# Cosine attention and a highway layer on one core: a new order of the same operations

## The chip, the cores and the metric

The kernel runs on one core of a Trainium2 chip. The metric is the device time of one execution in microseconds (us); smaller is better.

## What is computed

Eight batches, twelve heads, 448 tokens, head width 64. Queries and keys are brought to unit length, the scores divided by `tau` (0.1), and softmax attention gives `x` of 3584 x 768. A highway layer follows.

```python
q_n = q / (np.linalg.norm(q, axis=-1, keepdims=True) + 1e-06)
k_n = k / (np.linalg.norm(k, axis=-1, keepdims=True) + 1e-06)
scores = np.matmul(q_n, k_n.transpose(0, 1, 3, 2)) / tau
attn = softmax(scores)
x = (attn @ v).transpose(0, 2, 1, 3).reshape(3584, 768)
H = np.maximum(x @ w_h, 0.0)
T = 1.0 / (1.0 + np.exp(-(x @ w_t + b_t)))
out = T * H + (1.0 - T) * x
```

## The kernel before

The twelve heads of a batch are worked on as six pairs (head p and head p+6). Pair p of batch b has the number s = 6b + p, from 0 to 47. The first 384 tokens of a head are its main part, the last 64 its tail. The names below are those that the code gives its operations; a reader needs them to follow the steps.

**Loads.** `ld6 qr b` and `ld6 kr b` (L315) bring the main part of a whole batch of q or k, cast to fp16, 576 KB in SBUF; they are issued by GpSimd on the software queue. Batch 0 comes in pieces on the same queue: `ld2` (pairs 1 and 2, 96 KB, two for q and two for k) and `ld3` (pairs 3 to 5, 144 KB, again four; both L322). Pair 0 has loads of its own on SP and ScalarE (`ldf`, `ldqa`, `ldka`; L301 to L309). The tails of q, k and v are `ldqt`, `ldkt`, `ldvt` (L330, L334, L340; two halves of 96 KB each), and `ldv` (L338) is the main part of v, 1152 KB; SP issues them, and ScalarE issues the two `ldkt` of batch 0. `ld wt`, `ld wh` and `ld b` (L345, L347) are the weights and the bias, on the software queue.

**Attention.** Squares of q and k (`sq2`, `sq3`, of the tails `sqt`; on ScalarE L374 and L400, from batch 1 on with the main part on DVE, L375) are folded on DVE (`fa`, `fb`, `fc`; L389, L391, L393), and two Newton steps (`nt`, seven instructions, L423 to L429) give the inverse lengths. GpSimd scales q and k of a pair (`qn s`, `kn s`, L493) and the tails of q (`qtn b`, L503); DVE scales the tails of k (`kb`, L512). PE transposes a pair (`turn s`, L528 to L533) and the tails (`tail3 b`, L548), DVE copies them from PSUM (`cpT s` L537, `cpt3 b` L552). Of the scores PE makes three chunks of the main keys (`qk s c`, L582) and one of the tails (`qkt s`, L595), ScalarE the exponentials (`exp s c` L588, `expt s` L599). Values are cast to fp16 by `vc b p` (L607) and, the tails, by `vtc b` (L613, two halves, on ScalarE). PE multiplies (`av s c`, `avt s`; L625 to L645), DVE divides (`rc s` L653, `ev s` L655) into `x`. Pair 0 of batch 0 has its own small versions of these steps (`first_pair`, names with `0 0`).

**Highway layer.** Four row groups g = 4b + i to a batch. `x` is transposed by the DMA engines (`xd6`, `xd3`, L677, issued by SP) in batches 1 to 6, and by PE (`xt6`, L682, with DVE's `cpx6`) in the first and the last. `ff4` and `ff3` are groups of matmuls with the bias and the two weights (L702 to L716); ScalarE does `th` (L730), DVE `hm`, `gt`, `gg` (L737, L744, L747), GpSimd the last sum `out` (L752; DVE in the last two groups), and SP stores (`st`, `sth`; L762, L758). Twenty `warm2` (L283) are two matmuls each on constants, whose result nothing reads.

**What sets the order.** Nothing is scheduled at run time. `plan` collects 1807 operations in the order of the code; the table `ORDER` is a permutation of them, and each engine runs its own in that order. `SLOTS` gives, for each buffer at its first use, its place in a ring (three for `qr`, `kr`, two for `kt`, `qt`, `vt`, `vr`, four PSUM banks `pB`, two `pS`). `URGENT` marks operations of GpSimd on which the next marked operation of DVE waits, since the two share a port. A wait follows from data, from a buffer that must be free, and from the semaphores of the transfers: the transfers of SP and ScalarE together have eight, those of GpSimd eight more, in turn, so that a transfer waits in its engine's queue until the eighth before it has landed.

PE runs three kinds of tile: whole ones, the 64-row tiles of `qk`, and the 64-column tiles of the last row group of a batch.

Of the kernel before, what the change touches and what calls it, by code (L numbers as in the profile page):

```python
# [20 lines left out]
19 16 15 25 18 17 4 20 21 26 23 22 3 27 1 35 28 13 296 39 31 11 34 5 10 40 30 33 41 24 42 29 43 2 32 44 102 7 0  # L21
90 45 57 46 47 291 96 48 49 9 50 91 51 8 292 59 87 52 60 53 101 58 38 54 97 6 36 61 99 89 37 85 62 94 63 92 293
88 12 294 64 65 66 56 67 68 69 55 70 71 112 103 295 106 86 113 130 110 108 109 111 107 129 14 117 72 298 121 104
119 105 118 73 131 122 299 95 120 74 98 132 115 149 116 75 140 93 516 148 134 138 76 114 100 139 77 150 133 521
78 190 124 141 123 79 80 126 152 135 125 81 171 136 82 297 151 137 168 127 153 128 159 167 154 155 144 300 169
156 142 170 186 157 160 145 143 305 209 513 317 172 306 178 83 158 146 187 147 179 161 307 514 163 173 301 188
176 308 174 302 177 84 518 189 205 175 309 193 303 164 194 191 304 206 162 197 192 318 207 198 310 195 208 180
515 196 311 165 216 319 212 217 200 312 320 213 210 181 313 321 201 211 214 166 199 202 215 314 183 322 315 182
203 316 204 334 337 517 218 184 219 220 323 185 221 329 222 223 336 332 260 324 242 355 261 224 333 262 243 729
331 263 244 325 330 264 247 225 732 356 338 326 229 728 327 339 520 248 328 374 230 249 343 393 341 344 357 226  # L30
432 358 342 227 375 231 235 228 245 431 378 366 246 376 413 367 364 377 345 412 236 346 433 238 414 522 527 365
381 434 250 394 237 528 251 944 382 532 347 232 415 335 362 360 529 340 233 736 252 348 265 530 731 256 363 234
385 730 395 533 386 266 519 361 523 352 253 396 397 379 383 359 534 349 380 254 531 350 524 733 384 368 370 535
369 351 435 255 400 267 417 239 271 418 525 371 257 390 401 272 536 258 387 353 416 398 273 402 399 526 734 389
388 268 240 354 403 436 391 372 269 392 437 404 537 442 270 405 440 419 538 748 443 278 408 441 406 539 409 540
407 541 423 420 279 438 542 410 280 543 411 439 552 281 373 550 551 421 447 424 445 545 446 422 444 546 283 282
448 544 553 555 449 426 612 554 425 571 549 547 427 548 428 742 570 560 429 743 558 430 284 559 589 450 572 285
561 590 556 573 562 557 948 738 591 581 467 737 563 577 579 593 592 564 627 580 565 1160 567 600 739 943 566 259
582 575 735 286 601 747 460 951 578 454 568 744 484 740 574 461 741 609 770 455 650 462 950 468 608 631 569 576
469 287 610 949 749 470 596 598 611 597 451 288 452 750 764 477 751 628 453 478 599 963 457 629 808 274 745 615  # L40
630 594 646 616 458 479 471 647 746 595 459 947 472 1158 752 765 584 753 501 953 586 473 585 474 846 754 275 456
619 755 583 620 475 756 757 827 758 634 476 613 276 635 648 587 488 649 614 604 588 605 766 602 638 632 639 759
617 603 633 489 786 606 945 607 494 618 289 463 495 767 490 651 496 636 491 761 637 1159 657 464 762 492 652 763
785 640 493 655 958 653 760 656 624 623 480 642 1162 952 658 768 622 946 654 769 621 842 643 1161 641 625 865
771 644 824 775 241 645 787 776 662 843 788 777 659 772 660 626 804 661 485 778 663 805 664 796 773 797 665 954
794 806 774 962 486 1165 844 795 807 823 781 682 779 845 782 465 780 809 783 790 784 502 791 481 503 789 1178
505 810 506 955 504 964 813 699 792 487 825 1168 793 672 965 686 1023 497 957 1177 687 814 673 507 482 966 811
688 849 812 798 826 815 800 959 799 850 483 508 669 1167 466 816 290 670 960 1163 674 979 801 862 666 1164 498
667 1169 671 675 668 509 689 956 499 676 961 690 716 802 803 832 830 833 510 683 691 500 677 700 831 861 511 847
1080 967 1374 692 968 1042 678 701 969 1172 1179 703 1373 848 970 1180 684 1173 971 1170 693 702 972 1174 704  # L50
685 973 694 980 863 1000 1181 834 705 709 981 864 851 828 1171 852 817 982 710 976 835 820 819 829 853 975 706
711 707 854 1378 974 818 985 1377 708 868 1001 872 821 869 1595 855 983 679 873 866 984 1039 870 867 858 822 856
1020 837 977 871 839 978 857 1038 1002 859 838 860 1019 986 990 1003 987 836 992 1057 840 876 841 874 991 877
1058 875 993 1007 878 1005 680 879 1008 1040 1021 880 1041 1006 1059 1011 1382 1009 1238 897 717 1219 712 1060
1010 1076 718 1022 720 512 719 1077 1166 721 1004 713 1012 1024 914 988 1175 1025 1078 1392 881 1079 1295 277
714 1016 989 1376 722 1015 1030 1176 1375 1047 1388 1049 1014 695 681 1589 1050 1013 715 882 1017 1048 1182 1018
890 1588 1031 696 1045 1043 1183 1046 995 723 1383 918 1044 994 1184 1393 997 996 883 919 1394 884 920 1384 1194
1064 1066 1185 1276 885 1186 1067 1187 887 998 999 888 1065 1188 724 898 1385 886 891 1196 1028 892 1026 725
1029 899 1386 915 900 1197 889 1027 1068 916 1191 904 1200 1395 1069 901 1190 1387 907 697 917 1083 1195 1062
902 1063 1380 905 1189 1593 903 908 906 931 1198 1215 909 1051 1052 1389 1053 1199 1054 1253 1591 921 1055 1084  # L60
1056 924 1216 925 1061 927 1192 1379 1254 1081 1193 1085 926 1590 1217 1086 1292 1073 1071 1592 1087 1082 1390
1070 1218 1234 1072 922 698 1088 910 1205 911 1089 1206 1035 1074 1034 1235 1075 1092 1033 923 1032 912 1222
1036 1203 1396 1223 1090 1091 1037 1236 1204 1255 1291 1093 1094 1207 1220 1237 1272 1201 1112 1221 932 1256
1273 933 1391 1202 1381 1598 935 934 1095 936 893 1208 1597 1243 1224 1274 937 1225 1211 1607 1226 1209 1244
1212 1275 1210 1241 1397 1227 1239 1398 1213 1245 1242 1214 1230 1113 1399 1603 1400 1231 894 1510 1228 1293 928
1257 1229 1246 1608 1594 1114 1240 1096 1294 726 929 1129 1232 1262 1233 1260 1263 1105 1599 1106 1115 727 1264
1261 913 1107 1097 895 1596 1302 1409 1248 1250 1303 1298 1277 1098 896 938 1247 1401 1099 1278 1402 1600 1249
939 1265 1100 1403 1406 1299 1122 1251 1116 1412 1252 1101 1410 1123 1411 1117 1124 1119 1431 1118 1283 1602
1136 1405 1415 1120 1284 1468 1133 1146 1121 1469 1102 1258 1300 940 1130 1301 1430 1137 1259 1134 1138 1404
1103 1135 1281 1609 1413 1282 1131 1604 1414 1269 1507 1132 1296 1279 1605 1297 1139 1601 1487 1407 1267 1280  # L70
1104 1268 1140 1610 1408 1432 1108 1266 1433 1449 1418 1416 1270 1419 1304 1141 1450 1470 1271 1306 1417 1422
1488 1471 1305 1285 1423 1611 1307 1420 1439 1308 1421 1288 1309 1451 1287 1434 1452 1441 1424 1442 1286 1109
1460 1706 1425 1606 1110 1489 1289 1440 1290 1426 1427 1461 1310 1437 1435 1142 1147 1436 1125 1428 1150 1506
1344 1429 1453 1151 1490 1438 1148 1612 930 1152 1477 1327 1458 1613 1126 1478 1445 1444 1614 1508 1615 1149
1143 941 1446 1459 1443 1111 1509 1311 1144 942 1475 1496 1476 1312 1153 1447 1345 1448 1497 1127 1348 1472 1349
1346 1350 1616 1617 1317 1154 1347 1618 1337 1630 1621 1313 1492 1494 1155 1318 1479 1319 1314 1626 1480 1334
1495 1620 1320 1668 1683 1315 1493 1321 1664 1335 1491 1361 1316 1627 1456 1336 1473 1625 1351 1322 1665 1474
1157 1338 1145 1331 1646 1457 1339 1666 1513 1667 1684 1454 1352 1455 1645 1628 1353 1332 1649 1629 1703 1482
1333 1498 1484 1687 1619 1354 1499 1355 1702 1328 1356 1622 1357 1329 1623 1481 1330 1483 1463 1485 1514 1647
1486 1517 1464 1721 1648 1624 1462 1465 1518 1358 1502 1675 1466 1515 1359 1676 1467 1511 1365 1512 1362 1516  # L80
1323 1366 1722 1363 1633 1364 1340 1631 1501 1634 1341 1503 1520 1324 1500 1632 1635 1325 1504 1522 1505 1636
1519 1637 1521 1638 1652 1523 1650 1524 1653 1685 1642 1367 1525 1656 1651 1686 1641 1704 1657 1669 1705 1559
1654 1723 1655 1639 1694 1640 1542 1670 1658 1643 1659 1644 1690 1671 1724 1326 1660 1672 1661 1360 1368 1526
# [794 lines left out]
```

## Time and profile before

| | us |
|---|---|
| median of three runs | 285.06 (284.66 to 285.47) |
| the profiled execution | 287.85 |
| its span, first to last instruction | 285.8 |
| PE busy with matmuls | 261.7 |
| DVE, ScalarE, GpSimd busy | 216.5, 207.6, 149.5 |
| mean granted TensorE clock | 0.98 |

The profile is of one execution. A line of a table names the line of the code, the engine and the tiles; times are from the start of the span. A busy PE is a PE with a matmul in flight; the clock is the share of full speed that the throttle granted. In the timeline the bracket at the end of a line tells how long the engine was idle before it and what released it.

### The profile page before, as it was taken

The numbers are of one execution on the slowest core, as the hardware profiler recorded it, in microseconds if no ns is written. First come the engines' busy times: TensorE is split into PE (matmuls) and PEld (weight loads), VectorE is DVE, ScalarE is ACT, GpSimd is POOL, SyncE is SP. The second block draws the span as 40 slices with busy tenths as digits, with TensorE's granted clock in tenths as the row PEclk, the third lists the DMA queues.
The fourth block names the chain that finished last, engine by engine and source line by source line (L and its number), as shares of the span: only waits on it lengthen the run. The fifth ranks groups of instructions, "written<-read, shape, count | busy, mean of one in ns | idle before, by whom it ended". The sixth has DMA issues, their size and how long they took to land.

```text
span 285.8 us, 8331 instructions
## 1 busy us (share of the span) xinstructions
PE 261.7 (92%) x3387; PEld 172.9 (60%) x3387; DVE 216.5 (76%) x516; ACT 207.6 (73%) x330; POOL 149.5 (52%) x163
## 2 busy tenths in 40 slices
PE   0839898999996999999999999999999999999992
PEld 0415566666653668655766577666865677567651
DVE  5669898499896779999899599966994577236474
ACT  3166990899994788868899867997887689772210
POOL 8623728824756366356863686366556751303260
PEclk9987999999999799999999999999999999999999
DMA  8999999999289919579949948480091104430243
GB/s 137 212 225 186 209 232 199 187 151 299 69 112 201 253 34 204 73 218 205 175 85 170 245 115 210 106 277 6 2 196 43 69 2 85 170 98 1 95 168 138
DMA packets 80150, 41.89 MB, mean 147 GB/s; under 512 B 61680, under 2 KB 77040, under 8 KB 80112
## 3 DMA queue, kind: packets, MB, share of 16 engines
q1 hardware_dynamic: 52864, 29.34, 42.3%
q0 software_dynamic: 26016, 11.60, 32.2%
q10 hardware_dynamic: 1232, 0.43, 0.7%
q8 instruction: 26, 0.43, 0.6%
q14 instruction: 12, 0.10, 0.1%
HBM read 37.82 MB, written 11.01 MB: 171 GB/s over the span
## 4 chain that ended last, share of the span: by engine, by line
PE 65%; DVE 20%; DMA 7%; issue 2%; POOL 2%; ACT 2%; SPq 1%; ACTq 0%; DVEq 0%; POOLq 0%
PE pB L716 26%; PE pS L582 9%; PE pB L629 7%; PE pB L711 3%; PE pB L645 3%; PE pB L595 3%; PE pB L528 3%; DMA kt<-in_k_dram 3%; DVE sq L375 3%; DMA vt<-in_v_dram 3%; PE pB L625 3%; DVE hm L737 2%; PE pB L705 2%; DVE f L389 2%; PE pB L530 2%
## 5 line engine op out<-in xcount | busy, mean ns | idle before, releaser
L588 ACT ACTIVATE E<-pS 128x896 f16<-128x896 f32 x144 | 127.4, 922 | 23.9 <-PE pS L582 21.7
L752 POOL TENSOR_TENSOR os<-x,hm 128x768 f32<-128x768 f16 (+1 forms) x30 | 43.9, 1468 | 68.9 <-DVE hm L747 37.4
L716 PEld LDWEIGHTS <-xT 128*128 128x128 f16 x576 | 52.8, 98 | 34.4 <-issue 5.4
L716 PE MATMUL pB<-wt,xT 128*128 128x384 f16 x288 | 60.4, 330 | 0.0
L716 PE MATMUL pB<-wh,xT 128*128 128x384 f16 x288 | 58.2, 327 | 0.4 <-DVE hm L737 0.3
L493 POOL TENSOR_TENSOR kp<-kr,rs 128x384 f16<-128x384 f16 x47 | 38.8, 831 | 26.9 <-PE pB L533 5.0
L493 POOL TENSOR_TENSOR qn<-qr,rs 128x384 f16<-128x384 f16 x47 | 38.8, 831 | 22.3 <-issue 5.7
L737 DVE SCALAR_TENSOR_TENSOR hm<-pB,x 128x384 f16<-128x384 f32 x56 | 30.6, 552 | 25.0 <-PE pB L716 23.5
L730 ACT ACTIVATE tt<-pB 128x384 f16<-128x384 f32 x56 | 27.3, 497 | 30.5 <-PE pB L716 27.2
L629 PE MATMUL pB<-vp,E 128*128 128x65 f16 x864 | 46.6, 194 | 0.4 <-ACT E L588 0.4
L582 PE MATMUL pS<-qT 64*128 64x384 f16 x288 | 41.1, 332 | 0.7 <-DVE qT L537 0.3
L629 PEld LDWEIGHTS <-E 128*128 128x128 f16 x864 | 39.6, 98 | 1.6 <-ACT E L588 0.7
L537 DVE COPY qT<-pB 128x896 f16<-128x896 f16 x48 | 29.4, 618 | 9.9 <-PE pB L533 9.6
L625 PE MATMUL pB<-vp,Et 128*128 128x130 f16 x144 | 32.0, 222 | 0.1
L582 PEld LDWEIGHTS <-qT 64*128 64x128 f16 x576 | 18.0, 94 | 21.9 <-issue 14.4
L599 ACT ACTIVATE Et<-pB 128x512 f16<-128x512 f32 x48 | 28.8, 606 | 3.2 <-PE pB L595 2.4
L655 DVE SCALAR_TENSOR_TENSOR x<-pB,rd 128x448 f16<-128x448 f32 x48 | 29.8, 622 | 1.1
L582 PE MATMUL pS<-qtT,qT 64*128 64x64 f16 x282 | 27.2, 189 | 0.0
L607 ACT CAST vp<-vr 128x384 f16<-128x384 f32 x42 | 21.0, 527 | 0.1
L653 DVE RECIPROCAL rd<-pB 128x7 f32<-128x7 f32 x48 | 9.5, 200 | 15.2 <-PE pB L629 13.7
L528 PE MATMUL pB<-ident,qn 128*128 128x128 f16 x144 | 16.2, 222 | 2.7 <-ACT tt L730 2.6
L595 PE MATMUL pB<-qtT,qT 128*128 128x64 f16 x94 | 18.0, 193 | 0.2 <-DVE qT L537 0.2
(92 smaller groups left out, 422.8 us busy)
## 6 DMA issues: line engine op xcount, KB each, us to landing
vr<-in_v_dram SPq DMA_DIRECT2D x8, 1152.0 KB, 8.8
out_dram<-os SPq DMA_DIRECT2D x24, 384.0 KB, 3.1
qr<-in_q_dram POOLq DMA_DIRECT2D x7, 576.0 KB, 13.1
kr<-in_k_dram POOLq DMA_DIRECT2D x7, 576.0 KB, 10.7
qt<-in_q_dram SPq DMA_DIRECT2D x16, 96.0 KB, 6.2
vt<-in_v_dram SPq DMA_DIRECT2D x16, 96.0 KB, 6.9
out_dram<-os SPq DMA_DIRECT2D x16, 96.0 KB, 2.3
kt<-in_k_dram SPq DMA_DIRECT2D x14, 96.0 KB, 6.4
```

The costliest lines, as they stand in the source:

```text
L493: return e.tensor_mul(R("qn" if t == 0 else "kp", s).rearrange("l c ab d -> l ab c d"), rows(t, b, p, p + 1)[:, :, 0, :].rearrange("l ab ( ...
L537: op("DVE", f"cpT {s}", lambda: nc.vector.tensor_copy(R("qT", s)[:, :], R16(("T", ti))[:, 0:896]), key, r=[("B", ("T", ti))], w=[("qT", s)])
L582: ins = nc.tensor.matmul(dst, lhsT=qT[ln, 384 + 128 * c : 512 + 128 * c], rhs=rhs, start=True, stop=True)
L588: return nc.scalar.activation(R("E", s)[:, c, :, 0:448], R("S", 3 * s + c)[:, :, 0:448], AF.Exp, scale=inv_tau)
L599: op("ACT", f"expt {s}", lambda: nc.scalar.activation(R("Et", s)[:, 64:576], R("B", ("S", s))[:, :], AF.Exp, scale=inv_tau), key + 3, r=[( ...
L625: nc.tensor.matmul(U[:, 2 * c : 2 * c + 2, :].rearrange("p g e -> p (g e)"), lhsT=Et[:, 128 + 128 * c : 256 + 128 * c], rhs=vp[:, 6:8, :]. ...
L629: ins = nc.tensor.matmul(U[:, 2 * c + ab, :], lhsT=EF[:, j, 576 * ab + 128 * c : 576 * ab + 128 * c + 128], rhs=vp[:, 3 * ab + j, :], star ...
L655: op("DVE", f"ev {s}", lambda: nc.vector.scalar_tensor_tensor(out=R("x", b)[:, :, D * p : D * p + D], in0=U_()[:, :, 0:D], scalar=0.0, in1 ...
L716: ins = nc.tensor.matmul(P[:, 0:MH], lhsT=xT[:, cc, :], rhs=w_[:, cc, MH * mh : MH * mh + MH], start=st, stop=(cc == CC - 1))
L730: op("ACT", f"th {g} {mh}", lambda pi=pi, mh=mh: nc.scalar.activation(R("tt", g)[:, MH * mh : MH * mh + MH], R("B", ("P", pi))[:, 0:MH], A ...
L737: return nc.vector.scalar_tensor_tensor(out=R("hm", g)[:, MH * mh : MH * mh + MH], in0=R("B", ("P", pi))[:, 0:MH], scalar=0.0, in1=xs, op0 ...
L752: op(en, f"out{wd} {g}", lambda: eng.tensor_add(R("os", g)[:, 0:W], xall(), R("hm", g)[:, 0:W]), at + 0.1, r=[("gg", g), ("x", b)], w=[("o ...
```

## The change

The code is the same, operation by operation; the three tables are new. Of each the first lines, and the end of `ORDER`:

```diff
 ORDER = tuple(
-19 16 15 25 18 17 4 20 21 26 23 22 3 27 1 35 28 13 296 39 31 11 34 5 10 40 30 33 41 24 42 29 43 2 32 44 102 7 0
-90 45 57 46 47 291 96 48 49 9 50 91 51 8 292 59 87 52 60 53 101 58 38 54 97 6 36 61 99 89 37 85 62 94 63 92 293
+17 18 11 2 291 20 6 16 96 19 21 84 26 24 22 83 28 87 25 99 23 296 91 27 39 1 0 14 8 32 5 4 29 294 15 30 35 41 40
+34 42 10 33 3 43 38 7 44 45 31 46 60 47 48 59 49 292 50 13 51 55 52 57 56 9 53 58 54 106 92 61 112 62 94 63 88
...
-1798 1800 1802 1793 1801 1803 1804 1805 1806
+1802 1793 1801 1803 1804 1806 1805
 SLOTS = tuple(
-0000010010123100000000000001001001201020101301010021210221021011103101200100020221311202103111010200100020021101
+0001102030101000100010102020220012103031100010011201130302101310011212000020102210310311121000300121011101210202
...
 URGENT = frozenset(
-103 130 329 355 374 375 413 510 552 571 608 766 804 824 895 940 981 1019 1020 1038 1039 1057 1058 1127 1189 1254
+129 186 288 329 374 393 412 413 431 544 570 571 767 785 824 843 912 929 974 982 1020 1038 1039 1155 1197 1234
```

In names, the parts that matter below (one engine's list each, in its order):

| list | before | after |
|---|---|---|
| GpSimd, first | `ld2 qr` x2, `ld2 kr` x2, `ld3 kr`, `ld3 qr` x2, `ld3 kr`, `ident`, `ld6 qr 1`, `ld6 kr 1`, `ld b`, `ld wt`, `ld wh`, `qtn 0`, `kn 1`, `qn 1` | `ld6 qr 1`, `ld2 qr`, `ld2 kr`, `ld2 qr`, `ld2 kr`, `ident`, `ld3 kr`, `ld3 qr` x2, `ld b`, `ld3 kr`, `ld6 kr 1`, `qtn 0`, `qn 1`, `kn 1`, `kn 2`, `qn 2`, `qn 3`, `kn 3`, `ld wt`, `qn 4`, `kn 4`, `kn 5`, `ld wh` |
| ScalarE, first | `ldka`, `ldf`, `ldka`, `ldkt 0`, table, `sqm`, `sqa`, `ldkt 0`, `sq2` (q), `sqt 0` x2, `sq2` (k), `sq3` (q), `vtc 0` x2, `sq3` (k), `exp 0 1` | `ldf`, `ldka` x2, `ldkt 0` x2, table, `sqa`, `sqm`, `sqt 0` x2, `sq2` (q), `sq2` (k), `sq3` (q), `exp 0 1`, `sq3` (k), `exp 0 0`, `exp 0 2`, `expt 0`, `vtc 0` x2 |
| SP, first | `ldf`, `ldqa`, `ldqt 0` x2, `ldvt 0`, `ldkt 1`, `ldvt 0`, `ldv 0`, `ldqt 1` x2, `ldkt 1`, `ldvt 1` x2, `ldqt 2` | `ldqa`, `ldf`, `ldqt 0` x2, `ldkt 1`, `ldqt 1`, `ldvt 0` x2, `ldv 0`, `ldkt 2`, `ldkt 1`, `ldqt 1`, `ldqt 2` x2 |
| PE, first | 13 `warm2`, `turn 0`, `tail1`, `warm2`, `tail3 0`, `qk 0 1`, `qkt 0`, `qk 0 2`, `turn 1` | 6 `warm2`, `tail1`, `warm2`, `turn 0`, 4 `warm2`, `qkt 0`, `qk 0 1`, `warm2`, `tail3 0`, `qk 0 0`, `qk 0 2`, `turn 1` |
| SP, at batch 3 | `ldv 3`, `xd6 4`, `ldkt 4`, `xd6 5`, `ldqt 5`, `st 1`, `ldvt 3`, `ldvt 4`, `xd6 6` | `ldvt 3`, `ldv 2`, `xd6 4`, `xd3 7`, `ldvt 3`, `xd6 5`, `ldvt 4` |

On DVE the first lists hold the same clears, folds and Newton steps of batch 0 in another order: most clears now stand ahead of the first pair's folds, and the last Newton steps of batch 1 (`nt36 1`) behind `ev 5`.

## The prediction

> **What bounds the kernel now.** I read the page's busy line and its slices first, then busy time by stage, then who waited for whom, then the timeline at the holes.
>
> ```profile
> PE 261.7 (92%) x3387; PEld 172.9 (60%) x3387; DVE 216.5 (76%) x516; ACT 207.6 (73%) x330; POOL 149.5 (52%) x163
> ...
> PE   0839898999996999999999999999999999999992
> ...
> PEclk9987999999999799999999999999999999999999
> ```
>
> TensorE is the bound, with three holes: the start, slice 13 and the end. In the stages (columns: stretch, length, busy us and count of each engine, clock):
>
> ```profile
> 14.20:46.10 31.90, 24.73 (x347) 15.56 (x346) 27.72 (x79) 23.59 (x33) 14.29 (x17) 0.89 1.25 214
> 46.10:80.00 33.90, 33.90 (x458) 22.50 (x458) 28.92 (x67) 29.63 (x49) 19.26 (x22) 1.00 1.05 174
> 80.00:98.50 18.50, 15.65 (x156) 9.47 (x153) 14.70 (x33) 13.12 (x25) 8.61 (x10) 0.91 1.17 196
> 98.50:280.40 181.90, 181.42 (x2409) 122.12 (x2406) 135.42 (x299) 137.64 (x219) 96.34 (x97) 1.00 0.56 123
> ```
>
> From 98.5 us on PE is full, and there each operation has one start-to-start time within 0.01 us: `av`/`avt` 0.25, `ff3` 0.49, `ff4` 0.65, `qk` 0.20, `qkt` 0.22, `turn` 0.39, `xt6` 0.33, and 0.10 more where the tile shape changes. Summed over all of PE's list without the warm-up matmuls (L283) this is 245.6 us. The last matmul ends at 280.3, so 34.7 us are lost before it: 28.5 until the first `ff4` starts at 46.1, 5.3 between 76 and 97.5, 0.9 elsewhere. Behind it stand 5.5 us of DVE and store.
>
> The middle hole, from the timeline (start, length, engine, line, idle before):
>
> ```profile
> 81.67 1.08 POOL L315 DMA_DIRECT2D qr<-in_q_dram  x1
> ...
> 82.19 1.60 SPq L762 DMA_DIRECT2D out_dram<-os  x1
> ...
> 83.84 1.50 SPq L340 DMA_DIRECT2D vt<-in_v_dram  x2
> ...
> 91.40 0.51 ACT L613 CAST vp<-vt 64x384 f16<-64x384 f32 x1 [3.57 <-DMA vt<-in_v_dram]
> 91.82 0.48 ACT L730 ACTIVATE tt<-pB 128x384 f16<-128x384 f32 x1
> ...
> 92.35 0.33 PE L528 MATMUL pB<-ident,qn 128*128 128x128 f16 x3 [2.58 <-ACT tt L730]
> ```
>
> A software load (`ld6 qr 4`) starts streaming; `ldvt 3 0`, issued 2.2 us later and behind a store, lands at 91.4, 7.5 us after its issue. The same load with an idle software queue (`ldvt 5 1`, 148.1 us) takes 2.7. ScalarE stands on it, the `th` behind that holds a PSUM bank, PE waits 2.6 us and then has half its clock for 3.4 us (1.7 lost). The start has the same thing:
>
> ```profile
> 6.59 0.62 ACTq L334 DMA_DIRECT2D kt<-in_k_dram  x1
> ...
> 14.38 0.52 ACT L400 ACTIVATE sq<-kt 128x384 f16<-128x384 f32 x1 [5.17 <-DMA kt<-in_k_dram]
> ...
> 15.67 0.76 DVE L389 TENSOR_TENSOR f<-sq 128x1152 f16<-128x1152 f16 x1 [3.42 <-ACT sq L374]
> ...
> 19.51 0.29 PE L533 MATMUL pB<-ident,first_kb 128*128 128x128 f16 x1 [4.85 <-DVE first_kb L474]
> ```
>
> The last `kt` load of batch 0 lands 7.8 us after its issue; the folds (L389) wait for the squares, and from 21 to 46 us DVE is nearly dense: it sets when the first `ff4` can start.
>
> **The change, term by term.** No operation is added or removed; so only the losses can move.
>
> *PE's own list.* The changes of tile shape fall from 174 to 169: 5 x 0.10 = **-0.5 us**.
>
> *Middle hole.* In the new order the two `vt` loads of batch 3 no longer stand behind a store: `ldvt 3 0` moves some 20 us of PE work ahead, `ldvt 3 1` stands before `ld6 qr 4` instead of behind it, 8.5 us of PE work before its `vtc` (before: 5.4). At the late price (7.5) it still arrives. I checked each load in this way, as PE work between issue and first reader: the shortest elsewhere are `ldqt 6 0` (3.0) and `ldkt 7 0` (3.1), both with no software load issued near before them (quiet price 2.7), and `ldqt 5 1` (7.0). Removed: 2.6 wait + 1.7 clock = 4.3, with the 0.1 of restart **-4.4 us**; the other 0.9 of this stage I leave. Bounds: 0 (another load is late in its place) and -5.3.
>
> *Start.* This is the disputed term. The software queue now begins with `ld6 qr 1`, of the next batch, ahead of batch 0's `ld2` and `ld3`. What is won: both `ldkt 0` are issued before the table load, so the 14.36 landing goes. What is late next: the `ld2 kr`, now fifth in its queue. In the trace that queue's 2560th packet starts at 13.2 us and all up to it have landed by 15.8; the new first 2560 packets are just `ld6 qr 1` (1536) and the four `ld2` (1024). I take 15.2, since the hardware queues have one gap as before; plus 0.84 (L374) the folds start at 16.0, **+0.3**. Bounds: 14.6, for DVE's own list of clears, first squares and Newton steps now standing ahead of the fold sums to 9.6 us after the first load lands (about 5); and 20.0, at the slowest 200 packets per us and 2.5 us of spread.
> The Trainium skill (DMA: Bandwidth & Descriptors, Anatomy of one DMA) gives a software transfer 2.0 us plus bytes over 436 GB/s, 3.3 us for this one. The trace's two such loads land 5.4 us apart (22.39, 27.83); by the page the start would be the third rival's, by the row it is mine.
> Behind the fold: three Newton steps' neighbours and two clears are moved away, so DVE needs 6.1 instead of 6.65 us up to `kb 0`; but `cpt3 0` now waits for `qkt 0`, `qk 0 1` and a warm-up pair ahead of `tail3 0` on PE, 2.5 us by the half-clock rows at 21 us, 1.3 at full; I take 2.0 where before 0.9 were idle. `kb 0` ends 8.0 after the fold's start (before 7.4): **+0.65**. From there to `cpx6 2` DVE has 24.3 us of work against 24.7: **-0.4**. PE has done 0.4 us less useful work when the first `ff4` starts: **+0.4**. Together **+0.9**. ScalarE does not overtake: `sq3 0 3 0` waits for `ld3 qr` (packet 3712, about 20.5), then 18 `exp` at 0.80, 6 `expt` at 0.48, two squares and four small ones fill 21.3 us to 41.8, where the last `exp` ended at 42.6 before. Behind `ldkt 2 0`, which waits for `kb 0`, `ldqt 1 0` and `ldkt 1 0` now queue on SP: issued about 25.5, with the software queue idle by then (weights are issued after `kn 3`, about 31), landed by 29, read at 31. The weights themselves move back by 20 us of time: `wh` lands about 47, its first reader is at about 50.
>
> *New small waits.* The first transposing load (L677) of a batch has 3.1 to 3.5 us of PE work before its reader in four batches, where it had 3.8 to 5.4; from issue to landing four of the six took 2.7 to 3.0, the others 3.4 and 4.3. **+0.5**, from 0 to 3.
>
> *End.* The last eight PE operations and DVE's last seven are the same: 0.
>
> Sum: -0.5 - 4.4 + 0.9 + 0.5 = **-3.5 us**. The profiled execution took 287.85 with a span of 285.8; the sum is made on that span (282.3 after), and I take the same 3.5 off the median of the runs, 285.06: **281.5**.
>
> **Rivals.**
> 1. *The lateness only changes its place.* Another hardware load meets a stream; `ldvt 3 1` has 1 us to spare. Then the 4.4 stay: 285.9. For it: 14 software loads of a whole batch still stream, most of them while SP has loads to issue, and one late load is enough. Against: the margins above, and a wait under half a us does nothing, since ScalarE is idle 27% of the time.
> 2. *Slower: the next batch's load in front starves the first batch.* Place: `sq2`, then `sq3 0 3 0` on ScalarE, with `exp 0 1` queued behind it. It decides from the moment the `ld2` land later than 14.8; each us later is a us of start. At the high bound the fold starts at 20.0 instead of 15.67, +4.3, with `cpt3` and the missing PE work +1.0, and `wh` behind them all reaches PE late by some 2 us: -0.5 - 4.4 + 7.3 + 0.5 = +2.9, 288.0.
> 3. *Better start.* The hardware transfers being late leave the engines to the software queue (440 packets per us alone against 280 shared): the fold starts at 14.6 (-1.1), PE is at full clock (-0.7), no new waits: 285.06 - 0.5 - 4.4 - 0.9 = 279.3.
> 4. *It does nothing to the lateness*, that is, the 7.5 us has another cause than the stream: the middle stays, the start costs 0.9: 285.5 to 286. The row against it is 2.7 at 148 us against 7.5 at 84.
> The Trainium skill (same page, Specifications) prices the first byte on SP's and ScalarE's path at a fixed 0.6 us; by that rule nothing here is late behind a stream and the change has nothing to count in. The row differs.
>
> **Numbers.** A change within 0.3% (0.86 us) can't be told from none. Forecast 0.50 (all faster); better start 0.18 (faster); moved lateness 0.12 and no effect on it 0.03 (two thirds of this within 0.3%, the rest slower); starved start 0.17 (0.15 slower, 0.02 still faster). So faster 0.70, same 0.10, slower 0.20. The range holds forecast, better start and moved lateness: 278.7 to 286.2.
>
> **What would show it.** Right: PE full from 80 to 98 with clock 1.00; no idle of ScalarE before L613; the first L389 near 16.0; the first L716 near 46.6; the chain of waits passing `qr`/`kr` loads, not `kt`, in the start. Wrong: L374 on ScalarE waiting for `qr` or `kr` beyond 17 us; the first L716 past 48; any PE wait over 1 us behind L677, L613 or `wh` after 48.

## The result, and the profile after

The changed kernel takes **288.99 us** (median of 4 runs, 288.69 to 289.51), the kernel before beside it on the same chip 285.18 (284.66 to 285.47): ratio 1.0118, 95% interval 1.0083 to 1.0154. It is slower by 3.8 us; the forecast was 281.5, its range ended at 286.2. The profiled execution took 289.51, with a span of 287.6.

The page of the changed kernel, its busy line and two rows of slices (7.2 us each):

```profile
PE 261.5 (91%) x3387; PEld 172.9 (60%) x3387; DVE 215.9 (75%) x516; ACT 208.5 (72%) x330; POOL 149.9 (52%) x163
...
PE   5078899999977999999999999799999999999992
...
PEclk9569999999995999999999999999999999999998
```

The hole that stood in one slice before now takes two (80 to 94 us), the clock row has its 5 there, and a new dent stands at 187 us. By stage (stretch, length, busy us and count of PE, PEld, DVE, ACT, POOL, clock, DMA share, GB/s):

```profile
14.20:44.80 30.60, 25.67 (x360) 16.82 (x360) 27.97 (x77) 24.18 (x36) 15.10 (x19) 0.92 1.24 224
44.80:80.00 35.20, 35.04 (x490) 23.23 (x488) 31.16 (x72) 29.76 (x48) 21.14 (x24) 1.00 1.10 178
80.00:98.50 18.50, 15.02 (x130) 8.41 (x128) 12.01 (x29) 11.82 (x23) 6.72 (x8) 0.82 0.96 124
98.50:180.00 81.50, 81.47 (x1146) 55.96 (x1145) 72.27 (x156) 69.66 (x109) 52.79 (x55) 1.00 0.83 168
180.00:190.00 10.00, 8.28 (x102) 5.37 (x100) 6.29 (x19) 6.96 (x12) 3.59 (x4) 1.00 1.02 273
190.00:281.50 91.50, 91.49 (x1163) 61.30 (x1162) 56.11 (x126) 61.89 (x100) 40.84 (x38) 1.00 0.27 71
```

From 80 to 98.5 TensorE did 130 matmuls at clock 0.82, where before did 156 at 0.91. Both dents have one name in the view of TensorE's waits (line, what it waited for, us in total, times, longest). Its first line belongs to the start; the second holds both dents:

```profile
PE pB L559 <- DVE first_qtn L469: 10.2, 1, 10.2
PE pB L716 <- DMA xT<-x: 5.2, 2, 3.5
```

`xT<-x` is the transposing load, L677. The timeline of the first wait (start, length, engine, line, idle before):

```profile
79.36 0.61 SPq L340 DMA_DIRECT2D vt<-in_v_dram  x1
...
79.63 1.08 POOL L315 DMA_DIRECT2D qr<-in_q_dram  x1
...
80.07 2.07 SPq L677 DMA_TRANSPOSE xT<-x  x1
...
88.04 1.14 PE L716 MATMUL pB<-wt,xT 128*128 128x384 f16 x3 [3.48 <-DMA xT<-x]
```

The v tail loads of batch 3 are early now, as the forecast has it. But the very next transfer on SP, `xd6 5`, is issued 0.44 us after the software load `ld6 qr 4` and lands (its data is in place) at 87.99, 7.9 us later. TensorE needs it and stands for 3.5 us, until 88.04; the clock is at half from 87.1 to 93.9. The second wait:

```profile
178.91 1.04 SPq L762 DMA_DIRECT2D out_dram<-os  x2
...
180.00 0.61 SPq L340 DMA_DIRECT2D vt<-in_v_dram  x1
...
180.71 0.79 SPq L762 DMA_DIRECT2D out_dram<-os  x1
...
181.60 2.67 SPq L677 DMA_TRANSPOSE xT<-x  x1
...
186.99 0.66 PE L716 MATMUL pB<-wt,xT 128*128 128x384 f16 x3 [1.72 <-DMA xT<-x]
```

Here `xd6 17` stands behind three stores and a v tail load on SP, and lands 5.3 us after its issue with no software load near (`ld6 qr 7` had landed at 164). Before, it went ahead of that batch's other transposing loads at 175.0 and took 2.8.

To compare kernels I use one measure: the start of a PE operation less all steady PE work ahead of it (by the start-to-start times of the prediction). What it grows by in a stretch is the time lost there, to waits and to half clock. "Middle" is from 50 to 68 us of PE work, "group 17" from 140 to 155.

| profile | PE's list | start | middle | group 17 | rest | all lost |
|---|---|---|---|---|---|---|
| before, first profile | 245.6 | 28.45 | 5.32 | 0 | 0.8 | 34.6 |
| before, second profile (`b_again`) | 245.6 | 27.26 | 4.86 | 0 | 0.8 | 33.0 |
| after | 245.1 | 27.56 | 6.44 | 1.97 | 0.9 | 36.9 |
| `a_xd5_early` | 245.1 | 27.37 | 0.06 | 1.83 | 1.5 | 30.7 |
| `a_xd5_vt_early` | 245.1 | 27.82 | 0.06 | 1.44 | 0.9 | 30.2 |
| `a_qr4_later` | 245.1 | 27.95 | 4.17 | 1.38 | 0.7 | 34.2 |
| `a_both` | 245.1 | 27.56 | 0.06 | 0.07 | 0.9 | 28.6 |
| `a_both_qr1_back` | 245.1 | 28.01 | 0.06 | 0.07 | 0.7 | 28.9 |
| `b_mend` | 245.6 | 27.71 | 0.82 | 0 | 0.8 | 29.3 |
| `b_vt3_early` | 245.6 | 27.66 | 1.48 | 0 | 0.8 | 30.0 |

With the 5.5 to 5.7 us behind the last matmul's start these give each span to 0.2 us. After against the second profile of before: -0.5 list, +0.3 start, +1.6 middle, +2.0 group 17, +0.1 rest = +3.5; the spans, 287.6 and 284.2, are 3.4 apart.

### The profile page after: what moved, and what is told of

The parts are those of the page before. It is cut to its first block, busy times and chain, and to the rows that moved or that the text cites. A ratio compares the mean times of both kernels' runs of the same rounds, so it can differ in the third digit from the quotient of the medians.

```text
span 287.6 us, 8318 instructions
## 1 busy us (share of the span) xinstructions
PE 261.5 (91%) x3387; PEld 172.9 (60%) x3387; DVE 215.9 (75%) x516; ACT 208.5 (72%) x330; POOL 149.9 (52%) x163
## 4 chain that ended last, share of the span: by engine, by line
PE 78%; DMA 9%; DVE 8%; ACT 2%; issue 1%; SPq 1%; POOL 0%; DVEq 0%; ACTq 0%; POOLq 0%
PE pB L716 33%; PE pS L582 11%; PE pB L629 8%; PE pB L711 5%; DMA xT<-x 5%; PE pB L645 4%; PE pB L595 3%; PE pB L625 3%; PE pB L528 3%; DMA vt<-in_v_dram 3%; PE pB L705 3%; PE pB L530 2%; DMA first<-in_q_dram 1%; DVE f L389 1%; DVE sq L375 1%; PE pB L682 1%
## 5 line engine op out<-in xcount | busy, mean ns | idle before, releaser
L716 PEld LDWEIGHTS <-xT 128*128 128x128 f16 x576 | 52.1, 99 | 38.5 <-issue 6.0
L716 PE MATMUL pB<-wt,xT 128*128 128x384 f16 x288 | 59.3, 328 | 5.2 <-DMA xT<-x 5.2
L716 PE MATMUL pB<-wh,xT 128*128 128x384 f16 x288 | 59.7, 334 | 0.0
L629 PE MATMUL pB<-vp,E 128*128 128x65 f16 x864 | 46.9, 194 | 0.0
L582 PE MATMUL pS<-qT 64*128 64x384 f16 x288 | 40.4, 330 | 1.3 <-ACT E L588 0.5
L537 DVE COPY qT<-pB 128x896 f16<-128x896 f16 x48 | 29.6, 619 | 14.6 <-PE pB L533 12.9
L599 ACT ACTIVATE Et<-pB 128x512 f16<-128x512 f32 x48 | 28.6, 602 | 5.9 <-PE pB L595 4.8
L582 PE MATMUL pS<-qtT,qT 64*128 64x64 f16 x282 | 27.3, 190 | 0.0
L645 PE MATMUL pB<-vp,E 128*128 128x65 f16 x288 | 18.4, 195 | 0.0
```

Source lines behind the costliest of these rows:

```text
L537: op("DVE", f"cpT {s}", lambda: nc.vector.tensor_copy(R("qT", s)[:, :], R16(("T", ti))[:, 0:896]), key, r=[("B", ("T", ti))], w=[("qT", s)])
L582: ins = nc.tensor.matmul(dst, lhsT=qT[ln, 384 + 128 * c : 512 + 128 * c], rhs=rhs, start=True, stop=True)
L599: op("ACT", f"expt {s}", lambda: nc.scalar.activation(R("Et", s)[:, 64:576], R("B", ("S", s))[:, :], AF.Exp, scale=inv_tau), key + 3, r=[( ...
L629: ins = nc.tensor.matmul(U[:, 2 * c + ab, :], lhsT=EF[:, j, 576 * ab + 128 * c : 576 * ab + 128 * c + 128], rhs=vp[:, 3 * ab + j, :], star ...
L645: ins = nc.tensor.matmul(U[:, 6, :], lhsT=lt, rhs=rh, start=(n == 0), stop=(n == 7))
L716: ins = nc.tensor.matmul(P[:, 0:MH], lhsT=xT[:, cc, :], rhs=w_[:, cc, MH * mh : MH * mh + MH], start=st, stop=(cc == CC - 1))
```

## The experiments

The theory, **A**: the time was lost because two transposing loads came late, one behind a software load's stream, one behind stores of its own queue; start and list have no part in it. Rival **B**: it is SP's own order, not the stream, that makes `xd6 5` late. Rival **C**: the loss lies in the start, with batch 1's q load ahead of batch 0's, or is spread. In `ORDER`, `xd6 4` is 450, `xd3 7` 501, `ldvt 3 1` 736, `xd6 5` 467, `ld6 qr 4` 943, `xd6 17` 1112, `ld6 qr 1` 291; the edits move such numbers and leave each tile in its buffer. They are shown by names, on one engine's list.

**The kernel before, profiled again.**

> The kernel before, unchanged, for a second profile of it. The profiled execution that the forecast was made on took 287.85 us, 2.8 above the median of its kernel (285.06). Theory A (the waits for late loads differ from execution to execution, and the first profile had a large one): the loss between 76 and 98 us is not 5.3 but 2 to 3.5 us, the span is 282.5 to 284, and the rest of the profile agrees with the first within 0.5 us. Rival (the middle hole is always 5.3): 5 to 5.6 us are lost there again, and whatever made the first profile long lies elsewhere.

Measured: 285.77 us, and 285.47 for the kernel before beside it (ratio 1.0024, 0.9992 to 1.0056), span 284.2. The middle lost 4.86, not 2 to 3.5. Its lines:

```profile
80.49 1.08 POOL L315 DMA_DIRECT2D qr<-in_q_dram  x1
...
82.47 1.75 SPq L340 DMA_DIRECT2D vt<-in_v_dram  x2
...
89.77 0.51 ACT L613 CAST vp<-vt 64x384 f16<-64x384 f32 x1 [3.13 <-DMA vt<-in_v_dram]
```

So the hole is there in both profiles, nearly as large as I took it. Of the 1.6 us by which the first profile was longer, 1.2 lie in the start. The theory's word on the hole falls; the rival is nearer, though 4.86 is a little below its 5 to 5.6.

**Group 5's transposing load first.**

```diff
 SP: ldv 2, xd6 4,
-xd3 7, ldvt 3 1, xd6 5,
+xd6 5, xd3 7, ldvt 3 1,
 ldvt 4 1
```

> The changed kernel with one move: on SP the transposing load of row group 5 goes ahead of that of group 7 and of the second v tail load of batch 3 (all three groups' x is ready at 76.7 us). Theory A (what counts is whether a transfer is issued before the software load of batch 4's q starts to stream, 79.6 us): group 5's load is issued at about 78.1, lands at about 81, and TensorE does not wait at the first L716 of group 5; but the v tail load is now issued at about 80.7, behind the stream, lands at about 88, and ScalarE's L613 (due at about 85 once the other wait is gone) waits some 3 us for it: part of the hole comes back, 284.5 to 287. Rival B (the order on SP's own queue is what makes group 5's load late): no late load at all, 282. Rival C (the loss of the change lies in the start or is spread): 288 to 289.

Measured: 283.34 us (282.07 to 284.63), 0.9912 of before (0.9871 to 0.9953). The timeline (three transposing loads in one row, then the software load, then two v tail loads):

```profile
76.51 3.95 SPq L677 DMA_TRANSPOSE xT<-x  x3
...
79.45 1.09 POOL L315 DMA_DIRECT2D qr<-in_q_dram  x1
...
80.51 3.42 SPq L340 DMA_DIRECT2D vt<-in_v_dram  x2
```

`xd6 5`, issued at 77.9, landed at 80.7, and the middle lost 0.06 us. One move of one transfer takes the changed kernel from 1.0118 to 0.9912 of before, 5.7 us by the medians. The time lies below A's 284.5 to 287. `ldvt 3 1` did land late, at 88.7, 8.2 us after its issue, as A said, but nobody waited: L613 on the other half of the tile ran at 87.5, before that landing. The reader of `ldvt 3 1` is the second L613, which in the changed kernel ran at 108. I had taken the wrong reader, here and in the prediction.

**The v tail load ahead too.**

```diff
 SP: ldv 2,
-xd6 4, xd3 7, ldvt 3 1, xd6 5,
+ldvt 3 1, xd6 4, xd6 5, xd3 7,
 ldvt 4 1
```

> The changed kernel with two moves on SP: the second v tail load of batch 3 goes ahead of the first transposing load of batch 1, where SP waits for x anyway, and group 5's transposing load goes ahead of group 7's. Theory A: both are issued before the software load starts to stream at 79.6; no wait at group 5's first L716 (3.5 us gone) and no half clock behind it (3.4 us gone): 289.0 - 6.9 = 282.1, with 281.5 to 283. Rival B (queue order alone): the same here. Rival C (start or spread loss): 288 to 289.

Measured: 282.85 us (282.77 to 282.92), 0.9902 of before (0.9868 to 0.9937). `xd6 5` landed at 81.2. C falls with this and the run above; A and B are not told apart yet.

**The same SP queue, the software load later.**

```diff
 GpSimd: qn 15,
-ld6 qr 4, kn 15, kn 17, qn 16, kn 16,
+kn 15, kn 17, qn 16, kn 16, ld6 qr 4,
 outh 3
```

> The changed kernel with one move: GpSimd issues the software load of batch 4's q behind the fourth of the following normalisations (about 88 us instead of 79.6); SP's queue is as in the changed kernel. Theory A (the stream makes the transposing load late): group 5's load, issued at 80.1 as before, lands at about 83 instead of 88.0, and both its wait and the half clock behind it are gone: 282 to 283. Rival B (SP's own queue order makes it late): it lands at 88 again, 289. Rival C (start or spread loss): 288 to 289.

Measured: 286.93 us (284.72 to 288.87), 1.0041 of before (1.0003 to 1.0080); by the number alone it is a miss. The timeline of its profiled execution tells why:

```profile
80.47 2.28 SPq L677 DMA_TRANSPOSE xT<-x  x1
...
88.09 1.08 POOL L315 DMA_DIRECT2D qr<-in_q_dram  x1
...
88.26 1.23 SPq L677 DMA_TRANSPOSE xT<-x  x1
...
96.41 2.10 PE L716 MATMUL pB<-wt,xT 128*128 128x384 f16 x6 [2.61 <-DMA xT<-x]
```

`xd6 5`, behind the same transfers on SP as in the changed kernel and issued at 80.47, now lands at 84.2 in 3.8 us instead of 7.9, and TensorE doesn't wait for it: the stream was the cause, and B falls. Of the 5.2 us over the 2.8 that this load took in `a_xd5_early`, 1.0 is left without the stream, which SP's order may account for. But the moved load now starts 0.17 us before `xd6 6`, which lands 8.1 us after its issue, and TensorE waits 2.6 us for that one. The lateness changed its place a second time.

**All three moves: the version that beats both kernels.**

```diff
 SP: ldqt 7 0,
-st 13, st 8, ldvt 7 0, st 12, xd6 17,
+xd6 17, st 13, st 8, ldvt 7 0, st 12,
 ldv 7
```

(with the two moves of `a_xd5_vt_early`)

> The changed kernel with the two moves that put batch 3's v tail load and group 5's transposing load ahead of the stream, and a third: group 17's transposing load goes ahead of the stores of groups 13, 8 and 12 and a v tail load on SP (it was the last of these five, and its x is ready at 174.1, long before it is issued). Theory A (group 17's lateness comes from standing behind three stores of one queue, with no software stream near): issued some 2.6 us earlier and with a landing in 2.8 instead of 5.3 us, its wait, 1.4 us in the profile of the kernel with two moves, is gone: 282.85 - 1.4 = 281.4, 280.9 to 282. Rival (the queue is slow there whatever the order, or the stores' own lateness then stops os or hm): 282.5 to 283.5.

Measured: **281.74 us** (281.35 to 282.53), 0.9864 of before (0.9831 to 0.9896). `xd6 17` was issued at 172.6 and landed in 4.4 us, in time. It did not land in 2.8 as expected: ahead of the stores it took 4.4, behind them 4.8 in `a_xd5_vt_early`. So the wait went because the load was issued some 2.6 us earlier; that standing behind the stores made it slow is not shown, and why it takes 4.4 to 5.3 us here is open. The two stages that had the dents:

```profile
80.00:98.50 18.50, 18.50 (x209) 11.58 (x206) 16.90 (x40) 17.36 (x32) 11.47 (x13) 1.00 1.09 167
...
180.00:190.00 10.00, 10.00 (x107) 6.27 (x106) 7.15 (x15) 8.37 (x16) 7.74 (x9) 1.00 0.67 150
```

TensorE is full in both, at full clock, with 209 matmuls in the middle stage.

**The start's reordered load put back.**

```diff
 GpSimd:
-ld6 qr 1, ld2 qr, ld2 kr, ld2 qr, ld2 kr, ident, ld3 kr, ld3 qr, ld3 qr,
+ld2 qr, ld2 kr, ld2 qr, ld2 kr, ident, ld3 kr, ld3 qr, ld3 qr, ld6 qr 1,
 ld b
```

(on top of `a_both`)

> The kernel with the three moves, with the start's reordered software load put back: the load of batch 1's q goes behind batch 0's seven loads instead of ahead of them all. Theory A (VectorE's own list, not the arrival of batch 0's loads, sets the first fold in the changed kernel: its fold starts at 15.4, the last of these loads that it needs lands at 14.15): batch 0's loads land 3 to 5 us earlier, and yet the first L716 of group 2 starts within 0.5 us of where it does in the kernel with the three moves; time within 0.6 us of that kernel. Rival (the forecast's second rival, that load in front costs the start): the first L716 and the whole time come 1 to 2 us earlier. Other side: batch 1's q, now at about 19 instead of 10 us, holds something of batch 1 back: up to 1 us later.

Measured: 281.68 us (281.55 to 281.92), the same as `a_both`. First the changed kernel's start, then that of this one (L374 on ScalarE are the squares of batch 0's first loads, L389 on VectorE the first fold):

```profile
13.40 0.84 ACT L374 ACTIVATE sq<-qr 128x768 f16<-128x768 f16 x1 [0.53 <-DMA qr<-in_q_dram]
...
14.23 0.84 ACT L374 ACTIVATE sq<-kr 128x768 f16<-128x768 f16 x1
...
15.43 0.75 DVE L389 TENSOR_TENSOR f<-sq 128x1152 f16<-128x1152 f16 x1
```

```profile
9.87 0.83 ACT L374 ACTIVATE sq<-qr 128x768 f16<-128x768 f16 x1
...
10.60 0.83 ACT L374 ACTIVATE sq<-kr 128x768 f16<-128x768 f16 x1
...
15.79 0.75 DVE L389 TENSOR_TENSOR f<-sq 128x1152 f16<-128x1152 f16 x1
```

The squares are done 3.6 us earlier, and the fold starts no earlier: VectorE's own list, dense up to it, sets the start. Its dense part begins when pair 0's q (`ldf 0`) has landed, at 5.53 and here at 6.17, and reaches the fold 9.9 and 9.6 us later. The forecast's second rival is refuted by this, though with little to spare: in the changed kernel the last square ends at 15.07, 0.36 us before the fold.

**The kernel before, with its own hole mended.**

```diff
 SP: xd6 4,
-ldkt 4 1, xd6 5, ldqt 5 0, st 1, ldvt 3 0,
+xd6 5, ldvt 3 0, ldkt 4 1, ldqt 5 0, st 1,
 ldvt 4 1
```

> The kernel before, with two moves on SP: the transposing load of group 5 and then the first v tail load of batch 3 go directly behind the first transposing load of batch 1, ahead of a k tail load, a q tail load and a store. Both are then issued by 81.5, before the software load (issued at about 80 to 81.7) has its first packets out. Theory A (the hole before has the same cause as the hole after, a load issued just behind the stream's start): the middle hole of 4.5 to 5.3 is gone or falls under 1: 285.3 - 4.2 = 281.1, 280.5 to 282. Rival (another load of that queue is then late and read at once): 284 to 286.

Measured: 282.80 us (282.51 to 283.24) beside 285.82 for the kernel before, 0.9900 (0.9862 to 0.9938). The middle stage:

```profile
80.00:98.50 18.50, 18.27 (x218) 11.86 (x218) 16.64 (x38) 16.97 (x29) 11.89 (x13) 1.00 1.17 207
```

The hole is gone but for 0.82 us, 4.0 less than in the second profile. The time fell by 3.0, less than the 4.2 I expected, and lies 0.8 above the stated range. For the kernel before only SP's list was changed: there a load behind the stream and a load late in its own queue are not told apart.

**Only the v tail load moved in the kernel before.**

```diff
 SP: xd6 4,
-ldkt 4 1, xd6 5, ldqt 5 0, st 1, ldvt 3 0,
+ldvt 3 0, ldkt 4 1, xd6 5, ldqt 5 0, st 1,
 ldvt 4 1
```

> The kernel before, with one move on SP: the first v tail load of batch 3 goes ahead of a k tail load, and so ahead of group 5's transposing load (issued 0.6 us later for it). Theory A: L613 on ScalarE has its v tail in time and the 2.6 us wait and the half clock go; but group 5's load, which had no slack to its first L716, is late by 0.6 to 3 us, more if the stream starts before it: 281.5 to 284. Rival (the hole is not due to this load): 285.

Measured: 283.15 us (282.64 to 284.56), 0.9917 (0.9883 to 0.9951). `ldvt 3 0` landed in 2.6 us, `xd6 5`, issued 0.83 us ahead of the software load, in 4.8; the middle lost 1.48: a wait of 0.9 us for `xd6 5`, and no half clock. As A said.

## Why the prediction was wrong, point by point

- **PE's own list, -0.5:** 245.6 to 245.1 by the same count and step times; no run isolates it.
- **Middle hole, -4.4:** the mechanism and nearly the size are right. Without the new late load the stage loses 0.06 us (`a_both`) where before lost 4.9 and 5.3. I read before's hole from its timeline; its second profile and the two mended kernels confirm it.
- **New small waits, +0.5 (0 to 3): the step that failed.** I weighed the loads of q, k and v against a stream, and of the transposing loads only the first of each batch, at their landing time without one. `xd6 5` is the third of its batch on SP. In the trace after it has 4.5 us of PE work between its issue and TensorE's wait (80.07 to 84.56), and a software load was put 0.4 us ahead of it: priced at the 7.5 that I used for the v loads, the wait would have been 3.0 (it was 3.5), with the half clock on top. The trace of before had the hint, which I used for `ldvt 3 0` alone: there `xd6 5`, issued 1.5 us ahead of the stream, took 4.5 us. `xd6 17` is the other: moved from first to third transposing load of its batch, it was issued behind three stores, too near its reader for the 5.3 us it took. Measured in place of 0.5: 6.4 (middle) + 2.0 (group 17) = 8.4.
- **Start, +0.9:** its sign isn't borne out. The five profiles with `ld6 qr 1` in front lose 27.4 to 28.0 us up to the first L716 (mean 27.65), the four with before's start 27.3 to 28.5 (mean 27.77): no difference that can be told. Batch 0's first loads landed at 14.15, not 15.2, the fold started at 15.43, not 16.0, and `kb 0` ended 7.1 us behind its start, not 8.0. My lower bound (14.6, at about 5 + 9.6) named the term that rules, VectorE's own list; it came to 5.5 + 9.9 = 15.4.
- **End, 0:** right.
- **The base:** the first profile of before is untypical by 1.2 us in the start. I took differences off the median, so little came of it.
- **Sum:** -0.5 - 4.8 + 0.3 + 8.4 = +3.4 on the second profile of before, against -3.5 forecast; the runs differ by +3.8. Mended, the changed order gives 281.74, close to the 281.5 that I forecast. That is in part luck: it is another kernel, and beside a before of 285.82 its change is -4.1, not -3.5.
- **Rivals:** the first (lateness changes its place) is what happened. It got a chance of only 0.12, and its price was too low, before's hole again: the new late load stands ahead of TensorE directly, and it has a companion at 187 us. Nor was it the load that I suspected: `ldvt 3 1` landed in 3.5 us and was read at 108. The second is refuted by `a_both_qr1_back`. The third (fold at 14.6, start shorter) didn't come; with the forecast's other terms of the start its price would add up to -1.15 (279.0), not -0.9. The fourth is refuted by `a_qr4_later`; the first-byte time that I set beside it says nothing of landings, and here these took 2.7 us quiet and 7.3 to 8.2 late. The line that was to show the forecast wrong, a PE wait over 1 us behind L677, is the one that came.

## What to carry to other kernels

When a change moves transfers around a streaming software load, list every transfer that is issued from about 1.5 us before that load is issued until its last packet, transposing loads and those deep in a batch too, and set the time to its first reader against the late price (7.3 to 8.2 us here), not the usual one (2.8). A load whose reader is far away costs nothing when it is late, one whose reader is TensorE costs its wait and, where that was 2.1 us or longer here, half clock as well: put the near readers ahead of the stream and let the far ones stand behind it. One swap on one queue was worth 5.7 us here, more than the mended order's whole gain over the kernel before (4.1 us, both by the medians).

## What the runs showed of the hardware

**How late depends on the distance to the software load.** Issue relative to the issue of `ld6 qr 4`, and issue to landing, in us, by the semaphore events of the traces:

| transfer, kernel | issue | landing after |
|---|---|---|
| `ldvt 3 0`, `b_vt3_early` | -2.22 | 2.56 |
| `xd6 5`, `a_xd5_early`, `a_both` | -1.53, -1.52 | 2.77, 2.75 |
| `xd6 5`, before (two profiles) | -1.51 | 4.51, 4.47 |
| `ldvt 3 0`, `b_mend` | -0.89 | 4.03 |
| `xd6 5`, `b_vt3_early` | -0.83 | 4.80 |
| `ldvt 3 1`, after | -0.27 | 3.49 |
| `xd3 7`, `a_xd5_early` | -0.25 | 5.63 |
| `xd6 6`, `a_qr4_later` | +0.17 | 8.10 |
| `xd6 5`, after | +0.44 | 7.93 |
| `ldvt 3 0`, before (two profiles) | +2.17, +1.99 | 7.54, 7.28 |

The stream itself begins later than the issue: the first packet of `ld6 qr 4` starts 1.8 us after it in seven of the ten profiles, and 2.4 to 3.3 us in the others. So a transfer issued 0.4 us behind the load is issued before any packet of it has moved, and is late all the same. The distance isn't all: at -1.5 the same load took 2.8 and 4.5 us (in before a k tail load went between it and the batch's first transposing load). Why is open.

**What the queues do meanwhile.** Packets that start in half a us, software queue and hardware queue, from the DMA records:

| us | after: software, hardware | `a_xd5_early`: software, hardware |
|---|---|---|
| 81.5 | 40, 12 | 34, 12 |
| 82.5 | 95, 16 | 200, 15 |
| 83.5 | 123, 112 | 240, 2 |
| 84.5 | 133, 135 | 241, 0 |
| 85.5 | 157, 116 | 38, 493 |
| 87.0 | 63, 415 | 15, 318 |

For about a us nearly nothing moves on either queue (a software packet takes 160 to 250 ns there, 50 later). Then in `a_xd5_early` the software queue has the engines nearly to itself for 2.5 us. Counted by packets, the data of `xd3 7` had all started by 82.5, and only 4-byte packets follow; but of `ldvt 3 1`, which SP had issued by 82.1, none starts until 85. In the changed kernel the two go one for one from 83 on, and the 256-byte packets of `xd6 5` get 270 a us, where `xd6 4` alone had 800 (400 in the half us from 78.0). The Trainium skill (DMA: Bandwidth & Descriptors, Queues, rings and completion order) says that each DMA engine takes turns between the queues it has work for, a packet at a time; the changed kernel's rows at 83.5 and 84.5 agree (123 to 112, 133 to 135), as do the us from 14 to 26 of the kernel before (211 to 209 in the us from 15, 283 to 280 in that from 21); the 2.5 us of `a_xd5_early` do not show it. What holds the hardware queue back there was not found out.

**The price of a wait is not its length.** The clock fell for 3.41 us after TensorE's waits of 2.1 (`b_again`) and 2.6 us (before, `a_qr4_later`), for 6.83 after 3.5 (after), and not at all after the 1.7 us at 187. So the wait of 3.5 us had twice the time at half clock of that of 2.6, and the waits of 1.7 and of 0.9 us (`b_vt3_early`) cost only themselves. Whether the length alone decides is not shown. In these traces every stretch at one clock that ends before the trace does is a multiple of 3.41 us long (68.27 us, 20 times that, ahead of the drop in before and after), and in the changed kernel the drop came 0.9 us ahead of the wait's end.
